# Another order by hand for the pieces of a transform and a first MLP

## The chip, the cores and the metric

The kernel runs on one core of a Trainium2 chip. The metric is the device time of one execution in microseconds (us), the median of several runs. Engines: TensorE (PE) multiplies, VectorE (DVE), ScalarE (ACT) and GpSimd (POOL) do the work between, SyncE (SP) issues the DMAs. Every engine takes its instructions strictly in the order in which the program gives them to it.

## The reference

```python
X = np.fft.fft(x, axis=1)            # x: (2, 3008, 256)
x = np.fft.fft(X, axis=2).real       # -> 6016 tokens of 256
h = x @ w_in                         # first MLP, d_ff 2048
x = (np.maximum(h, 0) ** 2) @ w_out
h = x @ w2_in                        # second MLP
out = (h * sigmoid(1.702 * h)) @ w2_out
```

## The kernel before, in words

A transform by matrices comes first, then two MLPs. A product in full precision is made of three in a reduced format: each operand is split into a high part (a rounded copy) and a low part (the rest), and high x high, high x low and low x high are summed in PSUM.

**Pieces.** The first stage, the transform and the first MLP, is written as small named operations, and the string ORDER lists all of them in the order in which they are issued. A name stands for a few instructions of one engine. There is no planner at run time: ORDER sets the queue of each engine, HOME sets which engine takes a piece that could run on several (V is DVE, A is ACT, G is POOL; without an entry the usual one), and RINGS says which buffer of a ring each new tile takes.

- `f0` to `f5`: six tiles of x are loaded (D), folded on DVE (s, a, p, m, u, v, w), multiplied by a feature table on PE (E, O), and copied to zc (e0, e1) and zs (o) on ACT, or DVE in the second batch.
- `e00`, `e01`, `e10`, `e11`, `o0`, `o1`: the transform over positions (E, N on PE), with copies and sums after it (c, s, n, m) and the split in high and low (h, l). It gives eight blocks of 376 or 378 token pairs. `c00` to `c13` load the tables for it.
- `i0` to `i3`, `u0` to `u3`: the groups of the first MLP's weights, loaded (D) as 64-bit words and made into high and low parts (A and L on ACT as a rule, C, S, O, P, M, N on DVE, H on ACT, l on POOL as a rule). `j` and `v` do it for the second MLP; `n`, `ny`, `nyq`, `se`, `ma` are small helpers.
- Each of 128 steps of the first MLP has `F` (six matmuls into two banks, L750 to L752), `P` (three DVE instructions that read these banks, L1040 to L1043), `R` (the squared ReLU: two on ACT, L1051 and L1052, or one on DVE, L1049), `H` (the high part, ACT, L1057), `G` (the low part, POOL or DVE, L214) and `B` (twelve matmuls into the accumulators, L765). The banks of F come from two rings of two, so F of a step waits until P of two steps before has read its bank. h has a ring of five, gh of five, gl of four.
- `X` copies the accumulators out at the end of a turn (after B3, B7, B15, ...) and stores them to DRAM; `Y` loads the part that an earlier turn has left.
- `y0` to `y3`, `yaH`, `yal`, `ybH`, `ybl` make the first operands of the second MLP. `yD` and `jlD` load for it.

The second MLP follows in code of its own with a fixed order (its matmuls are L1096 and L1112); the last four B of the first MLP lie in its first two units. Some of the memory on the left side is one temporary buffer (cv2) that e10, e11, j0, v0, o1, j1, v1 and y use one after the other.

The three instructions of P and the two places of the sum o0s1:

```python
V.scalar_tensor_tensor(out=p, in0=e128, scalar=w1n_t, in1=ps[:, 0], op0=mult, op1=add)   # L1040
V.tensor_tensor(out=h[:, 0], in0=p, in1=ps[:, 1], op=add)                                # L1042
V.tensor_tensor(out=h[:, 1], in0=p, in1=ps[:, 1], op=subtract)                           # L1043
V.tensor_tensor(out=e2[:, par], in0=a, in1=held[par][:, 1], op=add)                      # L713
V.tensor_tensor(out=e3[:, par], in0=a, in1=held[par][:, 1], op=subtract)                 # L714
```

Of the kernel before, what the change touches and what calls it, by code (L numbers as in the profile page):

```python
# [65 lines left out]
F25  # L66
F26 i3S R23 u2H i3L B19 u2l H22 P25 R24 H23 H24 R25 P26 i3O B20 B21 G22
F27 G23 i3P B22 B23 H25 R26 P27
F28 G24 R27 i3M G25 H26
# [1 line left out]
F30 i3l u3A P30 G27 H28 B24
F31 B25 P31 R29 u3O u3C u3S R30 G28
F32 R31 B26 u3P P32 H29 G29
F33 H30 f3a0 G30 u3H P33 B27 f3s0 H31
F34 R32 H32 B28
F35 R33 P34 H33 G31 P35 R34
F36 o03h B29 G32 P36
F37 G33 u3l P37 B30
F38 R35 H34 G34 o03l B31
F39 B32 R36 P38 B33 f3p f3m P39 R37 f3v H35 o03N f3u H36 o03n B34 R38 G35 f3w H37 f4D G36 f3E R39 f4a0 H38 f4s0 Y35 G37  # L80
H39 c11D f3e0 f3O B35 G38 G39 X35.0
F40 f3e1 X35.1 f3o
F41 f5D P40 R40 H40 P41 B36
F42 R41 P42
F43 Y39 f4m G40 B37 f4p B38 B39 H41 P43
F44 G41 X39.0 X39.1 B40 P44 R42 H42
F45 R43 f4u H43 P45 R44
F46
F47 P46 H44 f5a0 R45 j0D H45 G42 B41 G43 f4v B42 P47 c10D
F48 R46  # L90
F49 B43 f4w R47 G44 B44 P48 f3g P49 H46
F50 f4O f5s0 G45 f4o G46 f5p H47 B45 f4E B46 P50 G47 f4e1 R48 c13D B47 f5m f5u f5v f4e0 H48 R49 f5w H49 f5E Y47 R50 G48
v0D X47.1 G49 H50 f5e0 G50
F51 f5O X47.0 f5e1 B48 P51
F52 f5o P52
F53 P53 R51
F54 =x H51 G51 R52 B49
F55 P54 H52 P55
F56 R53
F57 H53 B50 P56 G52 G53 e10E P57  # L100
F58 e10c B51 R54 e10s P58 e10N e10h R55
F59 e10n e10m R56 H54 G54 e11E B52 R57 H55 e10l H56 R58 G55 e11c P59 B53 e11N e11s H57 e11n
F60 e11h R59 P60 G56 e11m B54 B55 j0L
# [17 lines left out]
F78
F79 G75 R77 B72 P78
F80 R78 H76 H77 P79 B73 H78 v0S
F81 P80 v0P G76
F82 j1D B74 P81 G77 P82 G78
F83 B75 v0H P83 R79 R80 o1E0 R81 v0l
F84 R82 H79 G79 P84 o1c0 B76 R83 B77 o1s0 o1E1 o1c1 B78 H80 G80 H81 H82 o1s1
# [2 lines left out]
F87 P86 P87 R85 B80 H85 j1C  # L130
F88
F89 G84 B81 R86 P88
F90 G85 B82 P89 H86 P90 j1S R87 o12N o12n R88 G86
F91 H87 R89 P91 B83 H88 G87 j1O R90 j1P
F92 j11 B84 H89
F93 G88 P92 j12 R91 P93 B85
F94 H90 B86
# [1196 lines left out]
```

## Time and profile before

| | us |
|---|---|
| median of 3 runs | 961.28 (960.48 to 961.42) |
| the profiled execution | 960.73 |
| its span | 959.0 |
| PE busy in the span | 946.6 (99%) |
| DVE busy | 701.3 (73%) |
| ACT busy | 581.2 (61%) |
| POOL busy | 261.8 (27%) |
| mean granted TensorE clock | 0.997 of full speed |

The span runs from the first to the last instruction of the trace; the execution's own time has 1.7 us around it. The first matmul of the second MLP starts at 462.0 us, the first of step F0 at 31.55 us. Busy shares are means over the span: the first stage has another mix than the second.

### The profile page before, as it was taken

To read this page: it belongs to the slowest core of one execution; us is meant where nothing else is said; L and a number is where in the kernel's file an instruction comes from. 1 tells how busy PE (TensorE), PEld (TensorE's weight loads), DVE (VectorE), ACT (ScalarE), POOL (GpSimd) and SP (SyncE) were. 2 spreads that over 40 slices of the span, in tenths; PEclk is the share of its full clock that TensorE was granted. 3 is DMA by queue.
4 is the path that set the end of the run, shared out by engine and by line. 5 is a ranking of instruction groups with operands and counts; after the bars stand their busy time and mean duration, and the time that the engine had idled before them with its cause. 6 is when DMAs were issued, how large, how long until landed. Compare 5 with 4: busy or idle time off the path is not lost.

```text
span 959.0 us, 12390 instructions
## 1 busy us (share of the span) xinstructions
PE 946.6 (99%) x4844; PEld 849.3 (89%) x4844; DVE 701.3 (73%) x919; ACT 581.2 (61%) x688; POOL 261.8 (27%) x161
## 2 busy tenths in 40 slices
PE   8999999999999999999999999999999999999997
PEld 8699899998999899999988888888888888888996
DVE  6899999887878686799698754664675575556553
ACT  3799887764795586666765654554464464455442
POOL 0556465533472436635205020020020002000000
PEclk9999999999999999999999999999999999999999
DMA  8324222630020002200220110020011001000001
GB/s 309 112 80 161 77 66 104 231 110 25 1 77 1 33 1 87 78 33 1 104 91 14 44 44 0 1 85 4 1 44 44 1 10 74 1 1 22 23 1 40
DMA packets 21899, 53.58 MB, mean 56 GB/s; under 512 B 3280, under 2 KB 15184, under 8 KB 19152
## 3 DMA queue, kind: packets, MB, share of 16 engines
q1 hardware_dynamic: 21840, 52.79, 15.9%
q8 instruction: 38, 0.62, 0.3%
q14 instruction: 21, 0.17, 0.1%
HBM read 37.36 MB, written 15.42 MB: 55 GB/s over the span
## 4 chain that ended last, share of the span: by engine, by line
PE 63%; DVE 1%; issue 0%; ACT 0%; DVEq 0%
PE psb L1112 27%; PE psc L1096 24%; PE psb L765 9%; PE psa L750 1%; PE psa L752 1%; PE psa L751 1%; DVE gl L214 0%; DVE h L1042 0%; DVE h L1043 0%; DVE g L1176 0%; DVE w L214 0%; DVE p L1040 0%; DVE h L1049 0%; DVE o L1202 0%; ACT o L1200 0%
## 5 line engine op out<-in xcount | busy, mean ns | idle before, releaser
L765 PE MATMUL psb<-gh,w 128*128 128x376 f32 (+1 forms) x1024 | 234.2, 335 | 1.1 <-DVE ue L714 1.0
L214 POOL TENSOR_TENSOR gl<-h,gh 128x752 fp32r<-128x752 f32 (+1 forms) x85 | 165.1, 1947 | 169.3 <-PE psb L765 65.6
L765 PEld LDWEIGHTS psb<-gh,w 128*128 128x128 f32 x1024 | 181.9, 189 | 2.7 <-issue 2.1
L1112 PE MATMUL psb<-gh,w 128*128 128x512 f32 (+1 forms) x576 | 163.7, 386 | 0.0
L1176 DVE TENSOR_TENSOR g<-u,psc 128x1024 f32<-128x1024 f32 (+1 forms) x48 | 57.6, 1200 | 116.3 <-PE psc L1096 116.3
L1057 ACT CAST gh<-h 128x752 fp32r<-128x752 f32 (+1 forms) x128 | 103.0, 818 | 53.4 <-PE psb L765 51.1
L765 PE MATMUL psb<-gl,w 128*128 128x376 f32 (+1 forms) x512 | 130.0, 335 | 0.0
L1178 ACT ACTIVATE g<-g 128x1536 f32<-128x1536 f32 (+1 forms) x48 | 70.4, 1468 | 94.2 <-DVE g L1176 94.2
L1112 PEld LDWEIGHTS psb<-gh,w 128*128 128x128 f32 x576 | 108.1, 188 | 20.6
L214 DVE TENSOR_TENSOR gl<-g,gh 128x2048 fp32r<-128x2048 f32 (+1 forms) x48 | 109.9, 2290 | 1.2 <-ACT gh L1153 1.2
L1051 ACT ACTIVATE h<-h 128x752 f32<-128x752 f32 (+1 forms) x106 | 88.1, 831 | 25.3 <-DVE h L1043 23.4
L881 POOL TENSOR_TENSOR ue<-raw 128x512 f32<-128x512 f32 (+1 forms) x11 | 23.7, 2169 | 254.1 <-DMA raw<-ydram 247.8
L765 PEld LDWEIGHTS psb<-gl,w 128*128 128x128 f32 x512 | 92.5, 189 | 0.0
L1040 DVE SCALAR_TENSOR_TENSOR p<-n,w1n_t,psa 128x376 f32<-128x376 f32 (+1 forms) x128 | 76.9, 601 | 19.9 <-PE psa L752 19.6
L750 PE MATMUL psa<-eo,w 128*128 128x376 f32 (+1 forms) x256 | 88.0, 344 | 3.0 <-DVE h L1043 2.3
L1052 ACT ACTIVATE h<-h 128x752 f32<-128x752 f32 (+1 forms) x106 | 88.7, 836 | 3.4
L1153 ACT CAST gh<-g 128x2048 fp32r<-128x2048 f32 (+1 forms) x48 | 90.3, 1882 | 0.1
L1042 DVE TENSOR_TENSOR h<-p,psa 128x376 f32<-128x376 f32 (+1 forms) x128 | 70.0, 547 | 25.2 <-POOL gl L214 6.4
L1112 PE MATMUL psb<-gl,w 128*128 128x512 f32 (+1 forms) x288 | 87.7, 386 | 0.0
L751 PE MATMUL psa<-eo,w 128*128 128x376 f32 (+1 forms) x256 | 85.6, 334 | 0.0
L752 PE MATMUL psa<-eo,w 128*128 128x376 f32 (+1 forms) x256 | 85.5, 334 | 0.0
L1175 ACT ACTIVATE g<-psc 128x512 f32<-128x512 f32 (+1 forms) x48 | 28.3, 590 | 77.6 <-PE psc L1096 77.6
(167 smaller groups left out, 1533.9 us busy)
## 6 DMA issues: line engine op xcount, KB each, us to landing
...
```

The source lines that it names most:

```text
L214: eng.tensor_tensor(out=o, in0=a, in1=f32(b), op=ALU.subtract)
L750: T.matmul(o, lhsT=w[:, 0, fs], rhs=t[:, par, 0, 0:wd], start=True, stop=False)
L751: T.matmul(o, lhsT=w[:, 0, fs], rhs=t[:, par, 1, 0:wd], start=False, stop=False)
L752: T.matmul(o, lhsT=w[:, 1, fs], rhs=t[:, par, 0, 0:wd], start=False, stop=True)
L765: T.matmul(acc[j][ec][:, s, 0:wd], lhsT=w[:, hl, e0:e0 + P], rhs=(gh, gl)[gi][:, s, 0:wd], start=(first and hl == 0 and gi == 0), stop=(la ...
L1040: V.scalar_tensor_tensor(out=p[:, 0:wd], in0=e128[blocks[j]][:, 0:wd], scalar=w1n_t[:, 0, f:f + 1], in1=ps[:, 0, 0:wd], op0=ALU.mult, op1= ...
L1051: A.activation(out=hv, in_=hv, func=AF.Relu)
L1052: A.activation(out=hv, in_=hv, func=AF.Square)
L1057: A.copy(st["gh"][:, :, 0:wd], st["h"][:, :, 0:wd])
L1096: T.matmul(bank, lhsT=w[:, hl, slot * P:(slot + 1) * P], rhs=x[:, yl, 0:wd], start=(first and hl == 0 and yl == 0), stop=(hl == 1), skip_g ...
L1112: T.matmul(o[:, s, 0:wd], lhsT=w[:, hl, e0:e0 + P], rhs=g[:, 2 * i + s, 0:wd], start=(f == 0 and hl == 0 and g is gh), stop=(f == 15 and h ...
L1153: A.copy(gh, gs[u - 1])
```

## The change

ORDER, HOME and RINGS are replaced by others. The operations are the same, each of them once, and what they compute is the same; the rest of the program isn't touched. What differs is the place of a piece in the queues, the engine of some pieces (`u1l`, `G23` to `G25`, `f4s0`, `f5s0`, `y1`, `y2`, `yal`, `y3` go from DVE to POOL, `u0L`, `e00c` and `v0L` from DVE to ACT, `u1L` and `X15.0` too; `i2l`, `G11`, `o0c1`, `R19` come to DVE, and others), and the buffers in the rings. The new order was searched for and judged by the mean of several layouts with delays drawn at random. The lines of which the text speaks (each line of ORDER begins where the F of that number is issued):

```diff
-HOME = {**dict.fromkeys("""j0L X3.1 X7.1 X15.1 X79.1 X95.1 X111.1""".split(), "A"), **dict.fromkeys("""f3s0 i1l i0l u0l i3l G44 G45 G50 G69 G71 G79 G101 G109 e01l o02l i2M i3M e10l e11l o13l y0 ybl0 ybl1""".split(), "G"), **dict.fromkeys("""f4s0 f5s0 u1l u3l G82 G99 u0L v0L v1L e00c e00n G5 u1L G8 G9 R12 G16 G17 X15.0 G22 G23 G24 G25 G28 G35 G37 G40 G47 G48 R54 e10n R56 G54 R58 G55 e11c R60 R62 G61 G63 j01 G64 G65 X63.0 G70 G74 G75 G77 G78 R80 R81 v0l o1c0 R83 o1c1 G81 R85 o12n G86 G87 G91 G92 R96 R97 R98 o13n G96 X95.0 R103 R104 R111 G112 R115 v1l R116 G114 G115 R117 R120 R121 G119 R123 G122 G123 G125 G126 G127""".split(), "V")}
+HOME = {**dict.fromkeys("""u0L j0L v0L X3.1 X7.1 X15.1 X63.1""".split(), "A"), **dict.fromkeys("""f3s0 f4s0 f5s0 i1l u1l i0l u0l i3l G44 G45 G71 G79 G99 G101 e01l o02l i2M i3M e11l o13l y0 y1 y2 yal y3 ybl0 ybl1""".split(), "G"), **dict.fromkeys("""u3l G50 G69 G82 G109 v1L e00n o0c1 G5 G8 G9 R12 G11 G16 G17 i2l R19 G22 G28 G32 G33 G35 G39 G40 G46 G47 G48 e10n e11n G57 R61 G62 R65 G63 R68 j01 j02 R74 G73 R76 G74 G75 R82 G80 G81 R85 X79.0 R86 R90 j1L o12n G93 R96 j13 G98 R100 o13n R108 G105 G108 R114 v1l X111.0 R122 R123 G122 G124 G125 R127 G126 G127""".split(), "V")}
...
-f0D f0a1 f0a0 nyD dfD f0s0 f0p ny f0s1 f0m f1D nD f1s0 f1a0 f1p nA f0E f1m f2D i0D i0A f1u f2s0 f2a0 f0O f2m f1O f2p f2u
-f1E nL f0e0 i0C seD i0L f0e1 f2E nC f1o i0O c00D u0D ma f1e1 f0o f1e0 i0S i0P f2O f2e0 f2o i0M i0N nO c03D se c01D i1D
-f2e1 nS e00E i0H e00N e01E u0L e00c i0l e00s e00h e00n f0g f1g e00l
-F0 u0A f2g e01c i1A e00m nP
-F1 P0 e01N e01s e01n
-F2 c02D e01h u0O u0C R0 P1 e01l o0E0 i1L e01m H0
-F3 u1D u0S R1 o0c0 u0P H1 P2 u0H
-F4 o0E1 R2 P3 G0
-F5 i1C P4 R3 H2 o0s0 o0c1 G1 i1S u0l u1A o0s1 i1O G2 o02h B0 P5 R4
-F6 H3 B1 P6
...
-F8 G4 u1C H6 B3 o02n i2D R7 G5 G6 P8 X3.0
-F9 X3.1 i1M H7 R8 u1L i1N
-F10 P9 i1H B4 P10
...
-F21 X15.0 X15.1 P20 u2O R19 G18
-F22 P21 R20 H19 R21 u2P B16
-F23 G19 P22 H20 i3C B17 H21 P23
-F24 P24 G20 R22 B18 G21 u3D
...
-F29 H27 Y23 i3N G26 X23.0 u3L P28 i3H X23.1 P29 R28
...
-F85 H83 G81 B79 G82 o13h o12h G83 =c X79.0
-F86 P85 o12l R84 X79.1 o13l H84 j1L j1A
...
-F100 H98 G98 P100 B95
-F101 j1H0 R99 X95.0 R100 X95.1 P101
...
-F127 B119 ybH0 R123 ybH1 G122 P127 R124 R125 B120 ybl0 ybl1 H123 B121 R126 H124 G123 H125 R127 B122 yal G124 H126 G125
-H127 B123 G126 G127
...
+f0D dfD f0a1 f0a0 f0s0 nD f0p f0E f0s1 nyD seD ny f1D f0m f1s0 f2D f1a0 i0D f0e1 nA f1m f0O u0D c00D f1p f0o nC f1u i0A
+f2s0 f2a0 f1E f2m f2p nL f1O nS f0e0 f2u f2E i0L ma f1e1 c01D i0C f2e0 i0O i0S se nO f1o f1e0 i1D i0P i0M i0N f2e1 f2O
+nP f2o u0A c03D u0C e00E i0H e00c e00N e00s u0L e00h e00n e00m i1A e00l c02D i0l e01E
+F0
+F1 e01c e01N i1L u0O e01s P0 f0g P1 e01h u0S R0 e01n e01l
+F2 u0P H0 R1 H1 P2 o0E0
+F3 e01m u0H i1C R2 f1g u1D f2g P3 o0c0 G0
+F4 H2 P4 o0s0 o0E1 o0c1
+F5 u0l G1 R3 o0s1 P5 H3 R4 u1A i1S o02h
+F6 B0 P6 i1O R5 B1 u1L R6 H4 G2 G3 H5 B2 i2D o02l u1C G4
...
+F7 i1P o02N H6 o02n P7 G5 B3
+F8 X3.0 P8 R7 X3.1 i1M u1O
+F9 u2D i1N B4 P9 R8
...
+F19 P18 u2C B14 H16 B15 i2N H17 G16 i2H R18 G17 i2l P19 u2L H18 R19 X15.1 X15.0 i3A
...
+F24 G20 u3D P24 i3S u2l
+F25 P25 H23 R24 G21 G22 B20 H24 R25 G23 j0D H25
+F26 Y23 P26 B21
+F27 G24 i3P P27 B22 G25 i3N
...
+F85 B77 v0P v1D R83 G80 o1E0 B78 P85 H81 G81 v0H H82 B79 R84 R85 v0l o1c0 G82 o1s0 X79.0
+F86 X79.1 o1E1 P86 o1c1 B80 R86 H83
...
+F101 H97 B93 G96 B94 P101 yD H98 G97 j1H1 B95 H99
+F102 G98 G99 R100 X95.0 j1H0 X95.1 P102 R101 B96
...
+F119 y0 y1 X111.0 H116 X111.1
...
+F127 B118 y3 R123 R124 ybl0 P126 B119 R125 G122 B120 H123 jlD P127 R126 B121 G123 H124 B122 H125 G124 G125 R127 ybl1
+H126 B123 G126 H127 G127
...
-    "h": "0123401234012340341203243102431430214302140231402314023140231024310243410234102341023410232341023410"
-          "234102341240312403124031241203412034120341203234102341",
+    "h": "0123401234012342401324120341203204132041342013420134204132041203412034103241032410324103242410324103"
+          "241032414103241032410324103102431024310243102024310243",
...
```

## Rows read from the trace of the kernel before

**Rows 1.** Table by stage: stretch, length, busy us of PE, PEld, DVE, ACT, POOL, clock, DMA.

```profile
0.00:31.55 31.55, 28.66 (x204) 26.28 (x204) 22.41 (x40) 13.57 (x37) 4.01 (x11) 0.95 0.75 280
31.55:52.00 20.45, 19.15 (x92) 13.77 (x91) 19.20 (x33) 16.84 (x23) 12.47 (x6) 1.00 0.18 62
52.00:146.00 94.00, 91.90 (x521) 89.02 (x520) 87.72 (x133) 85.34 (x108) 53.80 (x27) 1.00 0.29 98
146.00:462.00 316.00, 315.33 (x1824) 307.11 (x1825) 259.20 (x416) 215.31 (x278) 148.00 (x91) 1.00 0.17 59
462.00:959.00 497.00, 491.55 (x2209) 413.15 (x2207) 312.77 (x301) 250.17 (x245) 43.54 (x28) 1.00 0.09 31
```

**Rows 2.** Waits of the weight loads: us in total, times, longest us.

```profile
PEld psa L750 <- DVE h L1043: 5.4, 10, 0.7
```

**Rows 3.** PE's timeline: start us, length us, instruction, [idle before].

```profile
41.85 0.34 PE L752 MATMUL psa<-eo,w 128*128 128x376 f32 x1
42.45 0.44 PE L750 MATMUL psa<-eo,w 128*128 128x376 f32 x1 [0.26 <-DVE h L1043]
...
48.98 0.52 PE L765 MATMUL psb<-gh,w 128*128 128x378 f32 x2
50.54 0.59 PE L765 MATMUL psb<-gh,w 128*128 128x378 f32 x2 [1.04 <-DVE ue L714]
...
106.42 0.33 PE L752 MATMUL psa<-eo,w 128*128 128x378 f32 x1
107.18 0.44 PE L750 MATMUL psa<-eo,w 128*128 128x378 f32 x1 [0.43 <-DVE h L1043]
```

**Rows 4.** Timeline, DVE and POOL.

```profile
71.39 1.21 DVE L351 CUSTOM_DVE_ANT_0 ue<-ue 128x2048 uint16<-128x2048 uint16 x1
...
102.51 1.81 POOL L214 TENSOR_TENSOR gl<-h,gh 128x752 fp32r<-128x752 f32 x1 [3.91 <-ACT gh L1057]
...
102.64 2.76 DVE L351 CUSTOM_DVE_ANT_0 ue<-ue 128x2048 uint16<-128x2048 uint16 x1
```

**Rows 5.** Groups by line on DVE, 0 to 470 us: count | busy, mean ns | idle.

```profile
L214 DVE TENSOR_TENSOR gl<-h,gh 128x752 fp32r<-128x752 f32 x32 | 30.0, 948 | 5.8 <-PE psb L765 4.8 <-ACT gh L1057 1.0
...
L1049 DVE SCALAR_TENSOR_TENSOR h<-h 128x752 f32<-128x752 f32 x22 | 27.9, 1273 | 0.0
L351 DVE CUSTOM_DVE_ANT_0 ue<-ue 128x2048 uint16<-128x2048 uint16 x13 | 19.5, 1502 | 0.1
L345 DVE SCALAR_TENSOR_TENSOR ue<-raw,ue 128x1024 uint32<-128x1024 uint32 x13 | 16.6, 1279 | 0.0
...
L214 DVE TENSOR_TENSOR w<-ue,w 128x1024 fp32r<-128x1024 f32 x4 | 7.1, 1769 | 0.0
L518 DVE TENSOR_TENSOR t<-xt 128x1024 f32<-128x1024 f32 x5 | 6.3, 1250 | 0.0
...
L329 DVE TENSOR_SCALAR ue<-raw 128x1024 uint32<-128x1024 uint32 x4 | 3.2, 808 | 0.0
```

**Rows 6.** Timeline of the start, PE and ACT.

```profile
21.30 1.95 PE L577 MATMUL psa<-dft,xt 128*128 128x130 f32 x16
...
22.33 1.80 ACT L598 ACTIVATE zc<-psa,nyq 128x65 f32<-128x65 f32 x8
...
25.07 0.59 ACT L308 COPY zs<-psb 128x512 f32<-128x512 f32 x1 [0.94 <-PE psb L577]
...
26.13 1.43 PE L626 MATMUL psa<-cst,zs 128*128 128x189 f32 x8
...
26.56 1.07 ACT L395 CAST w<-ue 128x1024 fp32r<-128x1024 f32 x1
...
29.29 0.82 ACT L635 CAST eo<-ht 128x756 fp32r<-128x756 f32 x1 [1.66 <-DVE ht L667]
...
30.02 1.15 ACT L321 ACTIVATE ue<-raw 128x1024 f32<-128x1024 f32 x1
...
31.55 0.44 PE L750 MATMUL psa<-eo,w 128*128 128x378 f32 x1
```

More of the change, by code (lines that the diff above doesn't have):

```diff
@@ L60 @@
-F19 i3D R17 H17 B14 P18 i2M i2H R18 i2l B15 u2S G16 u2L
-F20 H18 G17 P19 i3A
-F21 X15.0 X15.1 P20 u2O R19 G18
-F22 P21 R20 H19 R21 u2P B16
-F23 G19 P22 H20 i3C B17 H21 P23
-F24 P24 G20 R22 B18 G21 u3D
[L66 to L69, printed above, removed]
-F29 H27 Y23 i3N G26 X23.0 u3L P28 i3H X23.1 P29 R28
[L71 to L103, printed above, removed]
@@ L121 @@
[L121 to L127, printed above, removed]
-F85 H83 G81 B79 G82 o13h o12h G83 =c X79.0
-F86 P85 o12l R84 X79.1 o13l H84 j1L j1A
[L130 to L137, printed above, removed]
@@ new lines @@
+F2 u0P H0 R1 H1 P2 o0E0
[6 more added lines that the diff above has]
+F9 u2D i1N B4 P9 R8
+F10 H7 i1H B5 H8
+F11 G6 R9 P10 G7 i1l P11 u1S G8 R10 H9 B6
+F12 G9 H10 f3D B7
+F13 G10 R11 X7.0 P12 u1P i2A X7.1 R12 H11 u1H i2C
+F14 G11 i2L B8 u1l H12 P13 B9 G12 R13 B10 u2A
+F15 i2O B11 H13 P14 i2S
+F16 R14 P15 i2P
+F17 G13 H14 P16 i3D B12 R15 H15 G14 R16 P17
@@ new lines @@
+F34 H31 P34 f3s0 G30 R33 B28 u3S H32
+F35 H33 P35 G31
+F36 R34 B29 G32 u3P G33 H34 R35 P36 f3a0 B30 u3H Y35 u3l o03h B31 H35 f3m G34
+F37
+F38 R36 f3p H36 B32 c11D G35 B33 P37 f4D P38 o03l R37 R38 B34 H37 G36 o03N f3u
+F39 f3v f3w o03n G37 B35 H38 P39 X35.0
+F40 X35.1 f3E R39 B36 P40 f4s0 H39 f3e1
+F41 f3e0
+F42 R40 P41 G38 R41 B37 P42 H40 G39 f3O R42
+F43 H41 G40 G41 H42 Y39 f5D f4a0 P43 B38 B39 X39.0 X39.1 f4p f4m
+F44 f3o
+F45 R43 f5s0 P44 B40 R44 P45
+F46 P46 H43 R45 R46 B41 H44
+F47 H45
+F48 G42 B42 P47 f4u G43 G44
@@ new lines @@
+F49 G45 B43 f4v P48 P49 H46 f4w f5a0 f5m B44 R47
+F50 G46 f5p R48 f4E H47 f4e0 H48 B45 G47 f4O f4e1 R49 P50 f4o R50 B46 H49 Y47 f5v B47 G48 f5u G49 f5w f5E X47.0 f5O f5e0
+F51 X47.1 f5e1 f5o
+F52 P51 P52 =x H50 R51 R52 B48
+F53 H51
+F54 P53 H52 P54 G50 G51 B49
+F55 R53 e10E e10c P55 e10s B50
+F56 P56 G52 R54 H53 e10h e10l e10N e11E R55 B51 e11c e11s e10n e10m R56 G53 H54
+F57 e11h H55
+F58 B52 P57
+F59 P58 G54 H56 e11l G55 R57 e11N H57 j0L G56 P59
+F60 e11n B53 c13D P60 G57
+F61 R58 e11m j0O j0A H58 P61
@@ new lines @@
+F62 B54
+F63 R59 B55 R60 P62 B56 G58
+F64 H59 v0D B57 G59 R61 R62 P63 H60 R63 H61
+F65 j0C P64
+F66 G60 P65 G61 B58 P66
+F67 H62 G62 R64 B59 H63 P67
+F68 H64
+F69 R65 B60 G63 B61 G64 f5g R66 j0S H65 P68 H66 B62 G65 R67 P69 B63 R68 j0P G66
+F70 X63.0 j01 j02 X63.1
+F71 B64 H67 H68 R69 j03 P70 j1D B65 G67 R70 P71
+F72 f4g P72 G68 H69
+F73 B66 H70 G69
+F74 P73 R71 j04 P74
+F75 G70 R72 j0H1 R73 H71 P75 B67
+F76 j0H0 j0l1 G71 B68 R74 f3g
+F77 H72 G72 P76 H73 B69
+F78 P77 G73 R75
+F79 H74 j0l0 B70 B71 v0L P78 v0A R76 v0O v0C G74 B72 P79 H75
@@ new lines @@
+F80 R77 G75 R78
+F81 H76 B73 R79 P80
+F82 G76 H77 P81 R80 H78 B74 G77 R81 P82
+F83
+F84 H79 G78 P83 B75 G79 H80 v0S P84 B76 R82
+F85 B77 v0P v1D R83 G80 o1E0 B78 P85 H81 G81 v0H H82 B79 R84 R85 v0l o1c0 G82 o1s0 X79.0
+F86 X79.1 o1E1 P86 o1c1 B80 R86 H83
+F87 o1s1 H84 H85
+F88 P87 R87 o13h B81 G83 P88 o12h G84 G85
+F89
+F90 H86 R88 B82 G86 P89 o12l o13l P90 H87 R89
+F91 B83 P91 H88
+F92 R90 o12N B84 R91 G87 P92 G88 H89
+F93 j1A j1L B85 P93 R92 G89
+F94 o12n =c H90
+F95 B86 j1O G90 P94 P95 R93 H91 B87
@@ new lines @@
+F96 B88 R94 H92 G91 H93 R95 j1C P96 G92 B89
+F97 j1S j1P G93 B90 j11
+F98 B91 R96 H94 j12 H95 P97 R97
+F99 G94 P98 R98 P99 H96 G95
+F100 j13 j14 B92 R99 o13N P100
+F101 H97 B93 G96 B94 P101 yD H98 G97 j1H1 B95 H99
+F102 G98 G99 R100 X95.0 j1H0 X95.1 P102 R101 B96
+F103 o13n H100 P103 H101 j1l1 R102
+F104 B97 G100 j1l0 H102 P104
+F105 G101 B98 G102 P105
+F106 R103
+F107 H103 R104 B99 R105 P106 P107 G103 R106 H104
+F108 v1L
+F109 P108 B100 R107 G104 B101 P109 H105 R108 R109
+F110 v1A G105
+F111 H106 B102 H107 G106 P110 B103
@@ new lines @@
+F112 G107 P111 B104
+F113 H108 R110 H109 B105 R111 P112 G108 P113 v1C
+F114 R112 v1O B106 H110 G109 H111 P114 v1S v1P R113
+F115 G110 B107 B108
+F116 v1H P115 G111 R114 v1l
+F117 R115 B109 H112 H113 B110 G112 G113 P116 H114 P117
+F118 H115 B111 R116 P118 G114 G115 R117
+F119 y0 y1 X111.0 H116 X111.1
+F120 B112 yaH G116 y2 P119 H117 R118 B113 R119 H118
+F121 G117 P120 B114 P121 H119 R120
+F122 B115
+F123 G118 ybH0 B116 R121 P122 H120 yal
+F124 P123 G119
+F125 R122 G120 B117 ybH1 H121 G121 P124 H122 P125
```

78 lines of the change are left out of this document (17 added, 61 removed).

## The prediction

> **What bounds the kernel now.** The table by stage comes first [rows 1]. TensorE (PE) is busy 99% of the stretch from 146 to 462 us and 99% of the second network after 462. In 52 to 146, VectorE (DVE) is busy 87.7 of 94.0 us and ScalarE (ACT) 85.3, with PE at 521 matmuls. By the spacing of two starts in PE's timeline (0.17 us for one of 376 columns) [rows 3], 521 matmuls are 89 us of the 94. PE's busy figure includes modelled ends, so lost time has to be read from start to start. Done that way over the stretch 31.55 to 462, the gaps over 0.12 us sum to 6.25 us: 0.43 and 1.21 before 52, 3.35 in eight gaps from 105 to 146, 1.16 in three gaps at 260, 334 and 428 (the first two and the second largest of the eight stand in [rows 3]). The waits of the weight loads put ten of them on the last instruction of P (DVE, L1043), 5.4 us by that count, which begins at the end of the load before [rows 2]. So what ends last in the first stage is DVE: F may not reuse its bank until P has read it. The other loss is the time before the first F at 31.55 us [rows 6].
>
> Why DVE is late there is seen one instruction earlier. The L351 at 102.64 took 2.76 us, where the one at 71.39 took 1.21; a POOL subtraction had begun at 102.51 and ran to 104.32 [rows 4]. The gap on PE at 106.42 to 107.18 follows [rows 3]. On average such hold-ups make L351 1.50 us instead of 1.21 [rows 4, 5].
>
> Everything after 462 (497 us) [rows 1] is the same code in the same order, so I carry it over unchanged. The number of PE instructions is unchanged too. The time can change in three places only: the start, the stalls up to 146, the stalls after.
>
> **The start.** Before: f2E starts at 21.30 and ends near 23.2; ACT copies f1e0 and f2e0 as one run of eight at 22.33 (1.80 us, so 0.8 for each four start to start, the first copy's lead-in aside), takes f2o at 25.07, and the sine half of e00E begins at 26.13; F0 begins at 31.55 [rows 6]. After: DVE reaches f2u with two small words of n more (0.15 us), so f2E ends near 23.3. But on ACT f1o and f1e0 now stand behind f2e0, which waits for f2E, and f2e1 stands ahead of f2o. From 23.3 the queue is f2e0 0.8, se 0.2, f1o 0.5, f1e0 0.8, f2e1 0.8, f2o 0.6, that is 27.0 for f2o's end (a zs copy is 0.59 long in the row at 25.07; 0.5 and 0.2 are the estimates for its spacing and for a copy of a quarter of its columns). The sine half begins near 27.15, 1.0 later. Then e00c, moved from DVE to ACT, stands behind u0A and i0H (1.15 and 1.07 long, some 0.1 less start to start [rows 6]): 28.95, 0.25 after its data. The rest (e00s on DVE, e00h 0.82 on ACT [rows 6], e00l on DVE) is as before, so e00l ends 1.3 later, at 32.4. Before, e00l was done 0.25 us ahead of F0, which followed e01E on PE; so F0 moves by 1.05, to 32.6. Moving nD, nyD and seD ahead of f1D costs SP about 1.1 us of issue; DVE does not reach f1 until 12.3 in either order, after six half-tile sums of f0 and the Nyquist sums, which cover it. If the cover is gone, 1.1 more. **Term: +1.05, bounds 0.3 (ACT has slack that I do not see) to 2.6 (the f1D delay and a longer wait of e00c both count).**
>
> From F0 to 52: P0 now stands behind u0O and e01s on DVE, so F2 waits about 0.3 for the bank that P0 frees. Against that, F6 goes before B0, and o0s1 goes ahead of i1S and i1O. Before, B0's second half waited 1.21 for o0s1 (the wait on L714 [rows 3]), which had i1S ahead of it on DVE; now F5 and F6, twelve matmuls or 2.1 us, lie in front of B0, and o0c1 and o0s1, three reads of 376 columns, are some 1.6. The 0.43 in F4 goes as well. **Term: +0.3 - 1.64 = -1.34, bounds -1.64 and 0.**
>
> **52 to 146.** I add each engine's queue between the end of P6 and P34, with the mean lengths of the trace, hold-ups included. Before: DVE 88.7 (the trace has DVE busy 87.7 from 52 to 146 [rows 1]), PE 86.1, so DVE's queue is 2.6 longer than PE's. What leaves DVE in that stretch: u1l to POOL 1.77, u1L to ACT 0.81, G23 to G25 to POOL 3 x 0.95, X15.0 to ACT (taken as a G, 0.95), and, shifted past P34, u3S 0.8, u3P 1.5, f3a0 1.25 [rows 5]. What comes: G11 0.95, i2l 1.77, R19 1.27, and i1O 1.28, which stood before P6 [rows 5]. Net 9.9 less 5.3, so 84.1 for DVE. PE has one F fewer, 85.1. DVE's queue is now 1.0 shorter than PE's. ACT falls from 90.2 to 87.0 (PE covers it because B lags F by four to six steps), POOL stays at 54. DVE is thus at PE's pace and no longer behind it: from P8 to P19 it still has 37.9 against 37.2. I leave 1.0 of the 3.35 standing for single hold-ups of 1.5 us that come when no lead is left. **Term: -2.35, bounds -3.35 (no stall) and 0 (the same stalls at other places).**
>
> **146 to 462.** DVE is busy 259 of 316 us, ACT 215, POOL 148 [rows 1]: there is room. Over the stage POOL takes 24 us more than before, DVE 17 less and ACT 9 more. The 1.16 of before go or move; against them stand three places where the order is tight: B4 behind X3.1, which ACT takes after R7; o1E1 behind o1s0, behind o1c0, behind v0l on POOL; and B96 with one F instead of two between it and B95. Each is bounded by 0 and by the largest stall of before, 1.21 [rows 3]. I take 1.2 for the three together. jlD comes at the end, but its buffer is free since v1O, and SP runs ahead, so its transfer still has some 20 us before its use. **Term: 0, bounds -1.1 and +2.5.**
>
> Sum: +1.05 - 1.34 - 2.35 + 0 = -2.65. The profiled execution took 960.73 us (span 959.0); less 2.65, 958.1. The median of the runs shown is 961.28, 0.55 above it; on that scale the forecast is 958.6.
>
> **The rivals.** *The stalls move instead of going.* DVE loses time to POOL: the thirteen L351 took 19.5 us in all where 13 x 1.21 would be 15.7 [rows 4, 5], and the 22 of L1049 took 27.9 where 22 subtractions of that width would be 20.9 [rows 5]: 10.8 us beside 218 us of POOL work [rows 1], 0.05 per us. I double it for the kinds not counted: with 24 us more of POOL work, 2.4 us more hold-up. Where DVE's lead is gone it lands on PE, and the gain shrinks to 0.25: 961.0. For it: the stretched instruction in front of the large gaps [rows 3, 4]. Against it: nearly all of the added POOL work (f4s0, f5s0, y0 to y3, yal) lies after P34, where DVE has room [rows 1]. The Trainium skill, SBUF — State Buffer, section "Who interferes with whom", says that a VectorE instruction with two SBUF inputs or in a two-port mode and a GpSimd instruction that reads SBUF exclude each other for the whole instruction, and that the later one blocks; the L351 at 102.64, 1.5 us longer beside a POOL instruction begun 0.13 us before, agrees, though the rule alone would give each edit that sends work to POOL a price that the added queues above leave out.
>
> *The start decides (slower).* If ACT's new order at the start costs the full 2.6, DVE begins P0 behind u0O and e01s some 3.9 us later than before. Its 1.0 us of margin up to P34 cannot make that good, so the stalls of 52 to 146 stay; the early ones give back 1.4, and the tight places after 146 cost 0.8 more: +2.0, 963.3 on the median's scale. It decides from an F0 after 34 us. For it: f2e0 demonstrably waits for f2E [rows 6]. Against it: the walk above finds 32.6.
>
> *More is won.* ACT's slack hides the start (0.3) and no stall is left up to 146: 0.3 - 1.64 - 3.35, some -4.7: 956.6. Against it: every engine stands within 1 us of PE's pace from P8 on.
>
> **How the numbers follow.** Forecast, a gain of 2 to 4 us: 0.46. More is won: 0.12. The stalls move, within the same: 0.32. The start decides: 0.10. About 0.2% (1.9 us) is what a measurement of this kernel can tell from no change: faster 0.58, same 0.32, slower 0.10. The range 956.2 to 961.9 leaves out the slower case and the far end of the larger gain.
>
> **What would show it.** Right: F0 near 32.6 with f2e0 waiting for f2E on ACT; no gap ahead of B0's second half; gaps from 52 to 146 of about 1 us together; the second network beginning near 459.3 instead of 462.0 and taking 497 again. Wrong: F0 at 31.6 or after 34; three or more gaps behind stretched L351 or L334 as before; ACT, not DVE, named in PE's waits; gaps over 1 us at B4, o1E1 or B96; or a second network that is longer because its first weights came late.

## The result, and the profile after

The kernel after takes 952.44 us (median, 952.10 to 953.02) where the kernel before took 961.35 in the same runs: ratio 0.991, 95% interval 0.9893 to 0.9927. That is 8.9 us faster; 2.65 were forecast, and 952.4 lies below the range. The profiled execution took 953.02 us with a span of 950.8, against 960.73 and 959.0.

The table by stage of after; it answers [rows 1], with the first step F at 31.64 us and the second MLP's first matmul at 454.34. Columns: stretch, length, busy us of PE, PEld, DVE, ACT, POOL, clock, DMA share, GB/s.

```profile
0.00:31.64 31.64, 28.77 (x205) 26.01 (x205) 22.14 (x41) 15.87 (x40) 3.59 (x7) 1.00 0.76 281
31.64:52.00 20.36, 20.36 (x104) 15.79 (x103) 18.49 (x32) 18.66 (x25) 15.03 (x12) 1.00 0.17 60
52.00:146.00 94.00, 94.00 (x545) 93.80 (x545) 87.59 (x136) 87.60 (x110) 58.57 (x28) 1.00 0.37 130
146.00:454.50 308.50, 308.22 (x1790) 301.06 (x1789) 245.95 (x396) 216.82 (x283) 160.21 (x98) 1.00 0.15 51
454.50:950.80 496.30, 491.49 (x2209) 413.14 (x2207) 311.82 (x301) 249.82 (x245) 42.80 (x28) 1.00 0.09 31
```

PE starts 545 matmuls from 52 to 146 where it started 521, with DVE as busy as before. In the next table "over pace" is the start-to-start time of all F and B beyond 1.035 and 2.068 us (the pace at which six and twelve of these matmuls follow each other when nothing is waited for), by the stretch in which they begin:

| us | before | after | change | forecast |
|---|---|---|---|---|
| F0 starts | 31.55 | 31.64 | +0.09 | +1.05 |
| over pace, F0 to 52 | 2.41 | 0.43 | -1.98 | -1.34 |
| over pace, 52 to 146 | 4.54 | 0.27 | -4.27 | -2.35 |
| over pace, 146 to the end of the stage | 2.81 | 1.38 | -1.43 | 0 |
| second MLP | 497.11 | 496.46 | -0.65 | 0 |
| span | 959.0 | 950.8 | -8.2 | -2.65 |

Of the last 0.65, 0.05 lies between the first and the last matmul of the second MLP (491.58 and 491.53 us) and the rest behind the last matmul, where the output is copied out and stored (5.52 and 4.94 us). The kernels below take 491.5 to 491.6 and 4.8 to 5.5 there, in no relation to their first stage; I count it as spread. F0 to the second MLP's first matmul (430.29 before, 422.70 after) is the measure used below, because F0 itself moves from run to run with the arrival of x.

The waits of the weight loads of after, 31.64 to 454.3 us (answers [rows 2]; us in total, times, longest). F now waits once for L1041, which is the last instruction of P (lines are two lower than before):

```profile
PEld psa L748 <- DVE n L306: 0.6, 1, 0.6
PEld psa L748 <- DVE h L1041: 0.5, 1, 0.5
```

PE's timeline of after, where B0 waited before and where the only wait over 0.3 us is left (answers [rows 3]):

```profile
50.09 0.51 PE L763 MATMUL psb<-gl,w 128*128 128x378 f32 x2
50.44 0.85 PE L763 MATMUL psb<-gh,w 128*128 128x378 f32 x4
51.13 0.51 PE L763 MATMUL psb<-gl,w 128*128 128x378 f32 x2
...
340.72 0.33 PE L750 MATMUL psa<-eo,w 128*128 128x376 f32 x1
341.32 0.44 PE L748 MATMUL psa<-eo,w 128*128 128x376 f32 x1 [0.28 <-DVE n L306]
```

A long DVE instruction beside POOL is still there. DVE, POOL and PE of after, 107 to 112 us (answers [rows 4]):

```profile
107.67 2.90 DVE L343 SCALAR_TENSOR_TENSOR ue<-raw,ue 128x1024 uint32<-128x1024 uint32 x1
110.48 0.60 DVE L1038 SCALAR_TENSOR_TENSOR p<-n,w1n_t,psa 128x378 f32<-128x378 f32 x1
```

```profile
107.66 1.83 POOL L212 TENSOR_TENSOR gl<-h,gh 128x752 fp32r<-128x752 f32 x1
```

```profile
109.92 0.33 PE L750 MATMUL psa<-eo,w 128*128 128x378 f32 x1
110.09 0.50 PE L763 MATMUL psb<-gh,w 128*128 128x376 f32 x2
```

Here 1.7 us are lost on DVE and none on PE: it passes from F to B at 110.09 without a wait, while the next P doesn't begin before 110.48. The groups by line answer [rows 5] (DVE, 0 to 470 us: count | busy, mean ns | idle):

```profile
L212 DVE TENSOR_TENSOR gl<-h,gh 128x752 fp32r<-128x752 f32 x29 | 29.9, 1038 | 7.0 <-PE psb L763 3.2 <-ACT w2i L438 2.6 <-ACT yc L886 1.2
L343 DVE SCALAR_TENSOR_TENSOR ue<-raw,ue 128x1024 uint32<-128x1024 uint32 x13 | 18.5, 1422 | 0.0
L349 DVE CUSTOM_DVE_ANT_0 ue<-ue 128x2048 uint16<-128x2048 uint16 x13 | 17.5, 1349 | 0.1
L1047 DVE SCALAR_TENSOR_TENSOR h<-h 128x752 f32<-128x752 f32 x14 | 16.9, 1210 | 0.1
```

The custom pieces are stretched less (1.35 instead of 1.50 us), L343 more (1.42 instead of 1.28). "Stretched" means longer than the shortest instruction of the same form. Over the first stage the instructions stretched by more than 0.3 us cost DVE 20.7 us (23 of them) before and 21.1 (22) after. So the gain isn't that DVE is disturbed less on the whole.

The start of after on ACT and PE (answers [rows 6]):

```profile
22.48 0.93 ACT L596 ACTIVATE zc<-psa,nyq 128x65 f32<-128x65 f32 x4 [1.84 <-PE psa L575]
23.47 0.61 ACT L306 COPY zs<-psb 128x512 f32<-128x512 f32 x1
23.95 1.79 ACT L596 ACTIVATE zc<-psa,nyq 128x65 f32<-128x65 f32 x8
25.54 0.68 ACT L306 COPY zs<-psb 128x512 f32<-128x512 f32 x1
...
29.63 0.82 ACT L633 CAST eo<-ht 128x756 fp32r<-128x756 f32 x1
```

```profile
21.28 2.05 PE L575 MATMUL psa<-dft,xt 128*128 128x130 f32 x16
...
26.22 1.43 PE L624 MATMUL psa<-cst,zs 128*128 128x189 f32 x8
...
31.64 0.44 PE L748 MATMUL psa<-eo,w 128*128 128x378 f32 x1
```

f2e0 begins at 22.48, in the middle of f2E (21.28 to 23.17); the sine half of e00E begins at 26.22, where 27.15 was forecast and 26.13 was measured before.

### The profile page after: what moved, and what is told of

It is laid out like the page before. It is cut to its first block, busy times and chain, and to the rows that moved or that the text cites. A ratio compares the mean times of both kernels' runs of the same rounds, so it can differ in the third digit from the quotient of the medians.

```text
span 950.8 us, 12392 instructions
## 1 busy us (share of the span) xinstructions
PE 942.8 (99%) x4844; PEld 849.8 (89%) x4844; DVE 686.0 (72%) x902; ACT 588.8 (62%) x699; POOL 280.2 (29%) x171
## 4 chain that ended last, share of the span: by engine, by line
PE 95%; DVE 2%; DMA 1%; ACT 1%; POOL 1%; issue 0%; SPq 0%; DVEq 0%; POOLq 0%
PE psb L763 27%; PE psb L1110 27%; PE psc L1094 24%; PE psa L748 4%; PE psa L749 4%; PE psa L750 4%; PE psa L624 2%; PE psb L624 1%; PE psa L575 1%; DMA xt<-in_x 1%; POOL gl L212 0%; PE psb L575 0%; DVE t L516 0%; DVE t L512 0%; DVE gl L212 0%
## 5 line engine op out<-in xcount | busy, mean ns | idle before, releaser
L212 POOL TENSOR_TENSOR gl<-h,gh 128x752 fp32r<-128x752 f32 (+1 forms) x91 | 176.7, 1949 | 161.1 <-ACT gh L1055 73.7
L1049 ACT ACTIVATE h<-h 128x752 f32<-128x752 f32 (+1 forms) x110 | 91.4, 831 | 21.7 <-DVE h L1041 19.7
L1050 ACT ACTIVATE h<-h 128x752 f32<-128x752 f32 (+1 forms) x110 | 91.9, 836 | 3.5
```

What stands on the lines that cost most here:

```text
L212: eng.tensor_tensor(out=o, in0=a, in1=f32(b), op=ALU.subtract)
L1049: A.activation(out=hv, in_=hv, func=AF.Relu)
L1050: A.activation(out=hv, in_=hv, func=AF.Square)
```

## The experiments

The theory at the outset was that of queues: where DVE's queue is longer than PE's, F waits, and the gain is the work that leaves DVE. What it became is told under "Only other buffers". Times are medians, with the ratio to the kernel before and its 95% interval in brackets; the kernel before, run beside each, took 960.4 to 961.0. Waits, over pace and stage lengths are read from one profile of each kernel.

**The parts of the change alone.** Engines (HOME) without the order, and the order with its rings without the engines.

```diff
 # e1_home_only: ORDER and RINGS of before
-HOME = {... "f3s0 i1l i0l ..." "G", "f4s0 f5s0 u1l u3l ..." "V"}
+HOME = {... "f3s0 f4s0 f5s0 i1l u1l ..." "G", "u3l G50 ..." "V"}
 # e2_order_only: ORDER and RINGS of after
-HOME of after
+HOME of before
```

> The old ORDER and RINGS with the new HOME. Theory Q (the stalls come from DVE's queue being longer than PE's between two steps, and the new ORDER shortens it where it matters): DVE's largest excess over PE up to P34 is 4.7 us here against 5.3 before and 0.7 in the changed kernel, later 2.5 against 2.1; so the stalls stay, 959.5 to 962. Rival H (what helps is which engine takes a piece): the changed kernel's time or near it, 952 to 955.

> The new ORDER and RINGS with the old HOME. Theory Q: largest excess up to P34 2.0 us, later 1.0, so 1 to 2.5 us above the changed kernel: 953.5 to 955. Rival H: no gain, 959 to 962.

Measured: 977.94 (1.0181, 1.0164 to 1.0198) and 981.66 (1.0224, 1.0206 to 1.0241). Both theories missed both. Single stalls over 0.2 us: 27 with 22.9 us together, and 31 with 26.5, spread over the whole first stage. The waits of PE in the engines-only kernel:

```profile
PEld psa L750 <- DVE h L1043: 9.5, 18, 1.0
PEld psa L750 <- DVE p L1040: 6.0, 7, 2.0
PEld psa L577 <- DVE xt L554: 3.6, 1, 3.6
```

The last one is f3E, which waits for the folding of f3: one DVE piece of it took 2.89 us, 0.68 in the kernel before, beside the sum f4s0 that had moved to POOL, and the next DVE sum that f3E needs 2.00 instead of 0.41. DVE and POOL of the engines-only kernel:

```profile
165.12 2.89 DVE L544 TENSOR_TENSOR xt<-xt 128x512 f32<-128x512 f32 x1
```

```profile
164.61 2.86 POOL L514 TENSOR_TENSOR t<-xt 128x1024 f32<-128x1024 f32 x1
```

Stretches of DVE instructions come to 39.2 us over the first stage here and 36.3 in the order-only kernel, where before has 20.7. Part of the stalls above is the clock: behind waits of 1.4 to 2.8 us the granted clock fell to half (1.2 of 2.4 GHz) for 3.4 us at a time, once in the engines-only kernel (at 104 us) and three times in the order-only one (at 131, 175 and 353). PE started 10 to 12 matmuls in such a stretch where 20 fit at pace, so I estimate 1.4 to 1.7 us lost in each. Order and engines only fit together, so their shares of the gain can't be had by taking one away.

**The halves in time.** One order up to F55, the other from there, rings dealt anew (each new tile goes to the buffer that has been free longest); and the kernel after with only the ring of h dealt so.

```diff
 # x1_new_then_old, against after
 F54 P53 H52 P54 G50 G51 B49
-F55 R53 e10E e10c P55 e10s B50
+f3g c13D v0D
+F55 P55
 ... as in before
 # x2_old_then_new, against before
 F54 =x H51 G51 R52 B49
-F55 P54 H52 P55
+H52 P54
+F55 R53 e10E e10c P55 e10s B50
 ... as in after
 # r1_rings, against after
-"h": "0123401234012342401324120341203204132041..."
+"h": "0123401234012342401324102341023024130241..."
```

> The new order and engines for all that it issues before F55 (some 205 us), the old order and engines for the rest; buffers of the rings dealt again, each new tile taking the one released first. Theory Q (stalls where DVE's queue exceeds PE's): no excess over 0.7 us up to P54, the old ones of 1.2 at P67 and 1.1 at P118 remain, so only the late stalls of before (1.2 to 1.6 us) come back: 953 to 954.5. Rival W (the two halves depend on each other, or the gain is spread over the whole stage): 956 or more.

> The old order and engines before F55, the new ones for the rest, rings dealt again. Theory Q: the excess of 5.3 us up to P34 stays, nothing after: the time of before less the late stalls, 958.5 to 960. Rival W: 957 or less.

> The changed kernel with only the ring of h dealt again (each new tile takes the buffer released first; the other rings come out as they were). Theory Q: no difference, 952 to 953.5. Rival B (stalls come from which buffer of h a step must wait for): 2 us or more slower.

Measured: 953.73 (0.9926, 0.9911 to 0.9941), 955.89 (0.9949, 0.9934 to 0.9964) and 953.44 (0.9922, 0.9907 to 0.9937). The first and third as expected: most of the gain lies before F55, and the rings of after are not what makes it. The second missed the queue theory's range and fell in the rival's: with the old early order it should have gained 1 to 2.5 and gained 5. Its over pace from 52 to 146 is 1.21 although the order there is that of before (4.54). What differs in that stretch is the buffers of h, and two stretched instructions at 107 and 137 us that are not there.

**The engines in the middle.** Six pieces taken off DVE in before, and six G put on DVE in after.

```diff
 # e3_six_moves, against before
+HOME.update({'u1l': 'G', 'G23': 'G', 'G24': 'G', 'G25': 'G', 'u1L': 'A', 'X15.0': 'A'})
 # e4_six_back, against after
+HOME.update({'G10': 'V', 'G13': 'V', 'G14': 'V', 'G18': 'V', 'G19': 'V', 'G21': 'V'})
```

> The kernel before with six pieces off DVE (u1l and G23 to G25 to POOL, u1L and X15.0 to ACT), order unchanged. Theory Q: excess up to P34 falls from 5.3 to 2.5, so 2 to 3 us of the stalls between 52 and 146 go: 958 to 959.5. Rival B (the stalls come from the rings of h and from stores, or from when hold-ups happen to fall, not from DVE's load): 960.5 to 962.

> The changed kernel with six G of steps 10, 13, 14, 18, 19 and 21 on DVE instead of POOL (5.7 us more DVE work). Theory Q: excess up to P34 rises from 0.7 to 6.1 us, so 4 to 6 us of stalls come back between 60 and 150: 956 to 958.5. Rival P (POOL's hold-ups of DVE cause the stalls; six POOL instructions fewer): 951.5 to 953.

Measured: 959.85 (0.9985, 0.9975 to 0.9995), between the two theories; and 959.28 (0.998, 0.997 to 0.9989), which is 6.8 above after and a little more than the queue theory said. So a longer queue on DVE in this stretch does cost the gain; a shorter one alone doesn't bring it. Splitting the time between the ends of P6 and P34 on DVE shows why: work at its shortest, stretches (what instructions of that stretch take over the shortest of their form, from 0.3 us), idle.

| us | P6 to P34 | work | stretches | idle | over pace 52 to 146 |
|---|---|---|---|---|---|
| before | 91.05 | 79.46 | 5.58 | 6.01 | 4.54 |
| after | 83.80 | 75.17 | 2.80 | 5.83 | 0.27 |
| new order, then old | 83.83 | 75.06 | 2.80 | 5.97 | 0.31 |
| old order, then new | 87.30 | 79.55 | 2.20 | 5.55 | 1.21 |
| before, six moves | 90.57 | 74.11 | 8.54 | 7.92 | 4.08 |
| after, six back | 90.01 | 79.92 | 5.92 | 4.17 | 6.44 |
| before, ring of h dealt anew | 87.31 | 79.54 | 2.20 | 5.57 | 1.18 |
| before, six moves and ring | 88.57 | 74.12 | 7.39 | 7.07 | 2.27 |

Of after's 7.25 us, 4.3 are less work, 2.8 less stretches, 0.2 less idle time. The six G put back brought 4.75 of work and 3.1 of stretches, so what the work alone costs is not separated there. The six moves took off 5.35 of work and got 2.96 back as stretches and 1.9 as idle time.

**Only other buffers.** The theory of stretches: which instruction is stretched hangs on small shifts of POOL's starts, and the sum of work, stretches and idle time is what F waits for.

```diff
 # r2_old_rings, against before
-"h": "0123401234012340341203243102431430214302..."
+"h": "0123401234012340341203423104231023410234..."
 # e6_six_moves_rings: the same ring, and
+HOME.update({'u1l': 'G', 'G23': 'G', 'G24': 'G', 'G25': 'G', 'u1L': 'A', 'X15.0': 'A'})
```

> The kernel before (its order, its engines), with the buffers of the ring of h alone dealt differently (to the buffer that has been free longest). Theory H (what F waits for between P6 and P34 is DVE's queue, plus the stretches of single DVE instructions beside POOL, plus DVE's idle time; which instructions are stretched hangs on small shifts of POOL's starts): the stretches at about 107 and 137 us go as they did in the hybrid of the old early part with the new later part (2.2 us stretched instead of 5.6), the time over pace from 52 to 146 falls from 4.5 to about 1.2 to 2, and the median is 957 to 958.5. Theory Q (only the length of DVE's queue counts): the queue is the same, so 960.5 to 962.

> The kernel before with the six pieces moved off DVE (u1l, G23, G24, G25 to POOL, u1L and X15.0 to ACT), which gave 959.85, and the ring of h dealt as in the run beside it. Theory H (queue plus stretches plus idle): the six moves shorten DVE's queue by 5.35 us between P6 and P34, but gave back 3.0 us in longer stretches (8.5 instead of 5.6) and 1.9 in idle time; if the other buffers bring the stretches to 3 us or less, the time over pace from 52 to 146 falls below 1.5 and the median is 956 to 958. Theory Q: no change against the same moves with the old buffers, 959 to 960.5.

Measured: 957.00 (0.9967, 0.9957 to 0.9978), as the theory of stretches said: 3.6 us for the names of buffers. Work stayed as it was, stretches fell by 3.4 and idle time by 0.4 only, so it isn't mainly that DVE waits less for a buffer to come free. And 958.33 (0.9979, 0.9969 to 0.9989): stretches 7.39, not 3 or less, so the condition of its range wasn't met, while the queue theory's 959 to 960.5 missed as well. With the new ring the six moves cost 1.3 instead of gaining. How 0.2 us decides, first in before:

```profile
107.04 2.36 DVE L334 TENSOR_SCALAR ue<-ue 128x1024 f32<-128x1024 f32 x1
```

```profile
105.25 3.59 POOL L214 TENSOR_TENSOR gl<-h,gh 128x752 fp32r<-128x752 f32 x2 [0.93 <-ACT gh L1057]
```

and then with the other ring (lines are eight lower):

```profile
106.97 0.78 DVE L326 TENSOR_SCALAR ue<-ue 128x1024 f32<-128x1024 f32 x1
```

```profile
105.39 4.04 POOL L206 TENSOR_TENSOR gl<-h,gh 128x752 fp32r<-128x752 f32 x2 [1.03 <-ACT gh L1049]
```

POOL does two subtractions in a row. Before, the first ends where L334 is due (105.25 plus half of 3.59 is 107.04), the second goes ahead, and DVE's instruction ends 0.56 after it (109.40, POOL 108.84). With the other ring POOL is 0.14 later and DVE 0.07 earlier; DVE goes between the two (it ends at 107.75), and POOL's pair takes 4.04.

**Steps by hand.** Known causes removed in before one by one: o0s1 ahead of i1S, pieces off DVE ahead of the late stalls, or stretched pieces put elsewhere.

```diff
 # e5_by_hand, against before (ring of h dealt anew)
-F5 ... G1 i1S u0l u1A o0s1 i1O G2 o02h B0 P5 R4
+F5 ... G1 u0l u1A o0s1 i1S i1O G2 o02h B0 P5 R4
+HOME.update({**dict.fromkeys('u1l G23 G24 G25 G63 G114'.split(), 'G'), **dict.fromkeys('u1L X15.0 R62 R116'.split(), 'A')})
 # h1_three_places, against before (rings of before)
-F22 P21 R20 H19 R21 u2P B16
-F23 G19 P22 H20 i3C B17 H21 P23
-F32 R31 B26 u3P P32 H29 G29
+F22 u2P P21 R20 H19 R21 B16
+F23 G19 P22 H20 B17 H21 P23 i3C
+F32 R31 B26 P32 u3P H29 G29
```

> Steps by hand on the kernel before, without the searched order: the six moves off DVE, i1S put behind o0s1 (B0 no longer waits: 1.3), R62 and R116 to ACT and G63 and G114 to POOL (DVE's queue was longer than PE's by 1.2 before F69 and 1.1 before F120: stalls of .59 and .57 there), and the ring of h dealt differently. If the steps add: 1.3 early, 1.2 late and 2 to 3.5 in 52 to 146, so 955 to 956.5. If they do not add (a stall that goes is put back at the next bank by stretches), 957.5 to 960.

> The kernel before with three weight pieces of DVE at other places among their neighbours: u2P ahead of P21, i3C behind P23, u3P behind P32; same work, same engines, same buffers. These stood where a POOL subtraction had just begun and were stretched by 1.2 to 1.6 us each (at 102.6, 107.0 and 136.9 us). Theory H: if no other instruction is stretched in their place, 4 us of stretches go and the time over pace from 52 to 146 falls to 1 to 2: 957.5 to 959; if others are, the sum of queue, stretches and idle still gives the length from P6 to P34. Theory Q (queue only): 960.5 to 962.

Measured: 957.34 (0.9967, 0.9958 to 0.9976), between the two ranges and 0.2 below that of steps that do not add; it is no faster than the other ring alone (957.00). So the steps do not add. B0's wait went (over pace before 52: 2.41 to 1.13), but F69 and F120 still waited 0.48 and 0.54. At F69 the G63 that had left DVE stretched DVE from POOL (the pair at 252.51 and 253.53); DVE and POOL of this kernel (L343 is the custom piece, 1.21 at its shortest, as is L337):

```profile
249.78 2.21 DVE L337 SCALAR_TENSOR_TENSOR ue<-raw,ue 128x1024 uint32<-128x1024 uint32 x1
...
253.53 1.91 DVE L343 CUSTOM_DVE_ANT_0 ue<-ue 128x2048 uint16<-128x2048 uint16 x1
```

```profile
249.07 1.83 POOL L206 TENSOR_TENSOR gl<-h,gh 128x752 fp32r<-128x752 f32 x1 [4.28 <-PE psb L757]
252.51 1.86 POOL L206 TENSOR_TENSOR gl<-h,gh 128x752 fp32r<-128x752 f32 x1 [1.61 <-DVE p L1032]
```

At F120 the time freed by R116 and G114 came back as 1.10 us of idle time of DVE ahead of the next G.

The three places gave 958.25 (0.9982, 0.9972 to 0.9992), in the range, but not as expected: of the three, i3C is still stretched at its new place (1.62 instead of 0.68), and a sum of f3 that wasn't now takes 2.87 instead of 1.22; over pace from 52 to 146 is 3.0.

**The late stalls.** Each had one DVE piece of 0.7 to 1.2 us just ahead of the P that F waits for.

```diff
 # l1_late, against before with the ring of h dealt anew
-F66 G62 R64 B59 j0O R65 P66 j0P
-F67 H63 R66 G63 H64 P67 B60
+F66 G62 R64 B59 j0O R65 P66
+F67 H63 R66 G63 H64 P67 j0P B60
-F87 P86 P87 R85 B80 H85 j1C
-F89 G84 B81 R86 P88
+F87 P86 P87 R85 B80 H85
+F89 G84 B81 R86 P88 j1C
-F119 H115 R116 G114 G115 X111.0 H116 P118
+F119 H115 R116 G114 X111.0 H116 P118 G115
 # l3_two_late: the same without the move of j1C
 # l2_hand: l1_late, and i1S behind o0s1, u0P behind P2, u2P behind P22
```

> The kernel before with the ring of h dealt differently (957.0 so far), and three DVE pieces moved behind the P that they stood ahead of: j0P behind P67, j1C behind P88, G115 behind P118; same engines. Theory O (a late stall is one DVE piece of 0.7 to 1.2 us standing ahead of the P whose bank the next F but one waits for, with no lead left): the stalls at F69, F90 and F120 (0.57, 0.25, 0.57) go and none comes in their place, time over pace after 146 us 1.4 to 1.6 instead of 2.9, median 955.4 to 956. Rival M (the stall moves to the next bank): 956.6 to 957.4, with stalls of like size at F70, F91 or F121.

> The kernel before with the ring of h dealt differently (957.0) and only j0P behind P67 and G115 behind P118; j1C stays. Theory O (place of one piece): no stall at F69 and F120, F90 keeps 0.25, time over pace after 146 us 1.75 (of 2.88), first matmul of the second MLP's predecessor stage ends 425.9 after F0 (427.04), median 955.5 to 956.1. Rival M (such gains always come back at another bank): 427.0 after F0, 956.6 to 957.4.

> As the run beside it, with three more places changed early: i1S behind o0s1 (B0's wait of 1.3), u0P behind P2 (F4's .61) and u2P behind P22 (F24's .68); all pieces on the engines of the kernel before. If the steps add by their places alone: 957.0 less 1.4, 1.3, 0.6 and 0.6, so 952.8 to 953.8, near the searched order. Rival M (what is moved stalls the next bank, F5 or F25, or is stretched there): 954.5 to 956.

With all three moves: 956.13 (0.9952, 0.9936 to 0.9969), between the theories. F69, F90 and F120 no longer wait, but the stage is as long as before (427.01 from F0, against 427.04), because the F91 behind o12N now waits 1.1. DVE, POOL and PE of this kernel:

```profile
329.93 2.21 DVE L326 TENSOR_SCALAR ue<-ue 128x1024 f32<-128x1024 f32 x1
```

```profile
329.77 1.82 POOL L206 TENSOR_TENSOR gl<-h,gh 128x752 fp32r<-128x752 f32 x1 [2.28 <-PE psb L757]
```

```profile
333.08 0.34 PE L716 MATMUL psa<-eo,sel_t 128*128 128x376 f32 x1
334.36 0.44 PE L742 MATMUL psa<-eo,w 128*128 128x376 f32 x1 [0.94 <-DVE p L1032]
```

j1C, 0.68 long at its old place, now begins 0.16 after a POOL subtraction and takes 2.21. Without that move: 955.39 (0.9951, 0.9937 to 0.9965), 426.15 from F0, where 955.5 to 956.1 and 425.9 were expected; F69 and F120 do not wait, and 0.21 comes anew at F121. So two late stalls were the mere places of j0P and G115, worth 0.9 together.

With the early moves too: 956.72 (0.996, 0.9945 to 0.9974), a miss. F4 and F24 no longer wait and B0 waits 0.49 instead of 1.30, but F7 waits 0.70, F14 0.36 and F26 0.62 anew, and F0 to the stage's end is 427.05, the same again. The new wait of F7 has the same look:

```profile
50.03 2.83 DVE L337 SCALAR_TENSOR_TENSOR ue<-raw,ue 128x1024 uint32<-128x1024 uint32 x1
```

```profile
49.88 1.90 POOL L206 TENSOR_TENSOR eo<-ue,eo 128x752 fp32r<-128x752 f32 x1 [0.33 <-ACT eo L627]
```

That L337 is i1O, which now follows the moved i1S on DVE.

**Better than after?** The small Nyquist sums on POOL, and o13n on ACT; or o12n ahead of P93, since F94 waits for the bank that o12n reads.

```diff
 # v1_ny, against after
+HOME.update({'ny': 'G', 'o13n': 'A'})
 # a1_o12n, against after
+HOME.update({'ny': 'G'})
-F92 R90 o12N B84 R91 G87 P92 G88 H89
-F94 o12n =c H90
+F92 R90 o12N B84 R91 G87 P92 o12n G88 H89
+F94 =c H90
```

> The changed kernel with the six small Nyquist sums (ny, 0.87 us of DVE ahead of f2u) on POOL, and the copy o13n on ACT instead of DVE (PE's one stall of 0.43 us, at 341, names it). Theory S (the start is bound by DVE's queue up to f2u, and F0 follows it): F0 0.5 to 0.9 us earlier and the stall gone, 951 to 952. Rival: the start is bound by the arrival of x or by ACT, F0 unchanged, 952 to 953.

> The kernel after with o12n ahead of P93 instead of behind it (F94 waits for the bank that o12n reads) and the small Nyquist sums on POOL. Theory O: the stall at F94 (0.44 to 0.56) goes, first step F0 0.2 us earlier after x's arrival; first MLP's end 0.5 us earlier after F0, median 951.6 to 952.3. Rival M: P93 is later by 0.5 and F95 waits instead: 952.3 to 952.9.

Measured: 952.87 (0.9923, 0.9907 to 0.994), the rival's range, and 952.14 (0.9916, 0.9902 to 0.9931). In the first F0 followed the arrival of x 0.2 us sooner, not 0.5 to 0.9, and F94 still waited 0.56, so o13n is not what it waits for. In the second no F or B waits over 0.2 us, and F0 to the end of the stage is 422.35 instead of 422.70. Its median is the lowest of all, but 0.3 from after's, measured at another time, is not a measured difference.

## Why the prediction was wrong

The direction was right, and so was the place: DVE ahead of PE's banks, mostly in 52 to 146. Every term came out lower than forecast. Two sums of the prediction are off by little: its terms add up to -2.64, not -2.65, and its gaps to 6.15, not 6.25.

*The start (+1.05, measured +0.09).* The step that failed is "f1o and f1e0 now stand behind f2e0, which waits for f2E". f2e0 reads only the bank that the first half of f2E writes, so it began at 22.48, not at 23.3 behind f2E's end, and the queue behind it was that much earlier. The F0 of each run follows the first DVE instruction on x (7.49 us before, 7.76 after) by 24.06 in before and 23.88 in after. Ten other profiles with the start of before have 24.00, so the order itself won about 0.1. The first DVE instruction on x before, and after:

```profile
7.49 1.29 DVE L518 TENSOR_TENSOR t<-xt 128x512 f32<-128x512 f32 x2 [6.50 <-DMA xt<-in_x]
```

```profile
7.76 1.29 DVE L516 TENSOR_TENSOR t<-xt 128x512 f32<-128x512 f32 x2 [6.77 <-DMA xt<-in_x]
```

The rival on which the start decides rested on the same step and fell with it; [rows 6] show when f2e0 ran before, not what it waits for.

*F0 to 52 (-1.34, measured -1.98).* B0's wait and F4's went, as worked out (1.3 and 0.6 with what a stop costs behind it, see the next paragraph). The 0.3 for F2 behind u0O and e01s did not come.

*52 to 146 (-2.35, measured -4.27).* This term failed most, in two sizes. First the bound "-3.35 (no stall)": I had counted the gaps alone. A matmul that follows a stop takes 0.28 us to the next start and not 0.17 (107.18 to 107.45 in PE's timeline of before, behind the gap of [rows 3]), and there are smaller slips, so 4.54 stood to be won. The matmul behind the one at 107.18:

```profile
107.45 0.34 PE L751 MATMUL psa<-eo,w 128*128 128x378 f32 x1
```

Second, "I leave 1.0 of the 3.35 standing": 0.27 stayed. The forecast put DVE's queue 1.0 shorter than PE's and took single stretches of 1.5 us to break through. The 2.90 at 107.67 did come and cost PE nothing. After's stretches in P6 to P34 cost 2.80 us where before's cost 5.58. That pieces must leave DVE there is shown by the six G put back (6.44 over pace, through more work and more stretches); that the stretches count as much is shown by the ring of h alone (3.6 us with the same queue). The walk of mean lengths spread the stretches evenly and so could not see either. It forecast 4.6 less on DVE's queue, and DVE was busy 7.1 less (85.04 and 77.97). The queue itself was sized wrong: DVE was busy 85.04 of the 91.05 us in before, not 88.7, which is less than PE's 86.1. It is with the 6.01 of idle time, for which the prediction had no term, that DVE came out longer than PE.

*146 to 462 (0, measured -1.43).* The prediction expected the 1.16 of before to go and 1.2 to come back at three tight places. The step "I take 1.2 for the three together" failed: none of B4, o1E1 and B96 shows a wait of 0.2 us. Two of the three stalls were single pieces in a bad place (F69, F120: shown by moving them). After has one wait left, for o12n at F94 (shown by moving it).

*The rivals.* "The stalls move instead of going" was wrong for this change, and right for nearly each edit by hand: the six moves, the steps by hand, j1C and i1S gave back most or all of what they took, mainly through the mechanism that the rival named. The Trainium skill, SBUF — State Buffer, section "Who interferes with whom", calls that a lock between VectorE and GpSimd; the runs agree (DVE's instruction ends 0.55 to 1.1 us after POOL's in 107.04, 329.93, 50.03 and 107.67). I had charged it per us of POOL work, 0.05 and doubled; measured it goes by coincidence: POOL was busy 19 us more in the first stage, and the stretches came to 21.1 us instead of 20.7. "More is won" was the right case and still too small, since it took the same 3.35 as the whole and nothing after 146.

*What stays open.* Why this order keeps clear of the coincidences where the edits by hand did not: that it was judged under random delays would favour leads that survive a stretch, but no run here tells that apart from luck. Of the 17 to 21 us that the engines or the order alone lose, the stretches and the lower clock are seen, but the shares of stretches, idle time and clock were not taken apart.
